# Mask tables, a granule's work list, the last granule's products and two output stores rearranged in an attention-plus-MLP kernel

## The chip, the cores and the metric

The kernel runs on one core of a Trainium2 chip. The metric is the device time of that core in microseconds (us). Every kernel was executed several times; the first execution of each was also profiled (for the kernel before, one more execution beside the three that were timed). The time of an execution is about 1.8 us longer than the span that its trace shows (209.63 against 207.9 for the kernel before). All executions told of here are in the fast state, with a granted TensorE clock of 0.996 to 1.0.

## The reference, cut to what matters

```python
# q, k, v: (B=4, H=8, S=768, D=64);  n_global = 8, n_local = 96
scores = (q @ k.transpose(0, 1, 3, 2)) / sqrt(D)
keep = is_global | is_local            # first 8 keys, or 0 <= row - col < 96
scores = where(keep, scores - slope[h] * dist, -1e9)
a = softmax(scores)
x = (a @ v).transpose(0, 2, 1, 3).reshape(3072, 512)

h = x @ w_in                           # 512 -> 2048
g = s * maximum(h, 0)**2 + b
out = g @ w_out                        # 2048 -> 512, float32
```

## The kernel before

The 3072 rows are worked on in 12 *granules* of 256. For each granule PE (TensorE) makes the scores, ACT takes the Exp, DVE multiplies by a mask table (`tmpl`), PE makes the attention products, DVE normalises them into `xn`, and a transposing DMA makes `xT` of it (granules 4 to 11; for the earlier ones PE transposes it). Then come eight hidden-layer products `P1` (8 matmuls of 256 columns each, into one PSUM bank), ReLU on ACT, and a Square on ACT (`"act"`) or on DVE (else, or `"late"` with a later `Q`). The product with `w_out` is made plainly for granules 0 to 2 (`P2`), and as seven smaller products of sums and differences for the others (`W_mm`). Five PSUM pools matter: `psh` has two banks; `av`, `pso`, `scA` and `scB` serve one tile at a time.

The order of work is written by hand: each engine executes its instructions in the order in which the calls below issue them. The mask tables and their surroundings, before:

```python
    def make_tmpl(h):                          # a mask table: one Exp on ACT
        nc.scalar.activation(tmpl[:, h, :], base..., ACT.Exp, scale=slope)
    ...
    P1(1, 1)
    make_tmpl(2)
    P1(1, 2)
    make_tmpl(3)
    P1(1, 3)
    P1(0, 6)
    make_tmpl(4)
    T_quads(2, "k", ("pso", "av"))             # PE transposes k of granule 2
    T_ev(2, 0, "k")                            # evictions: DVE
    T_ev(2, 1, "k", "act")                     #            ACT
    P1(0, 7)
    T_quads(2, "q", ("pso", "av"))
```

One attention product `A`, with its normalisation, and the list that granules 3 and 4 are woven from:

```python
    def A(j, hp, tag="av", norm=True):
        ...                                    # 8 matmuls into a tile of pool `tag`
        if norm:
            A_norm(j, hp)                      # DVE: reciprocal, product into xn
            flush()                            # DVE: the Square that is pending

    def period(j, items, at, late=None, mid=()):
        SS(j, (0, 1))                          # scores and Exp
        run(items, at[0]);  A(j, 0)
        run(items, at[1]);  A(j, 1, "psh")
        run(list(mid), 100)
        SS(j, (2, 3))
        ...
        run(items, at[2]);  A(j, 2)
        KO(j + 1)                              # DVE copies of keys
        run(items, at[3]);  A(j, 3, "psh")
        if late is None:
            XT_dma(j)                          # two transposing DMAs, SP queue
        ...
        run(items, 100)
```

The last granule's seven products end with a product of eight 256-column matmuls, one addition on DVE and one store:

```python
        W_mm(j, 4)
        W_post(j, 4)
        nc.sync.dma_start(W_rows(j)[:, 1, lo], o[:, 1, lo])
```

The softmax here doesn't subtract the row's maximum and nothing guards it: scores larger than these inputs give would overflow.

## Time and profile before

| what | value |
|---|---|
| time, median of 3 executions | 210.44 us (210.06 to 210.52) |
| time of the execution that was traced | 209.63 us |
| span of the trace | 207.9 us |
| last matmul of the last product starts | 203.83 us |
| last store issued / landed / span ends | 204.66 / 206.53 / 207.86 us |

The lines of the profile on which the argument rests are in the prediction below, with how to read them. In the chain of waits the columns are start, duration, and what the time was spent on. In the order of time of one engine, a number in square brackets is the idle time before the instruction and names who ended it.

### The profile page before, as it was taken

Reading aid. Unit: us, or ns where it says so; the run is one execution under the profiler, and the core shown is the slowest. Engines: PE = TensorE matmul, PEld = TensorE weight load, DVE = VectorE, ACT = ScalarE, POOL = GpSimd, SP = SyncE. Lnnn points to the kernel's source line nnn. Section 1 sums busy time; section 2 is a strip of 40 time slices with the busy share of each in tenths; the row PEclk is TensorE's granted clock in tenths of the full one; section 3 lists DMA queues with packets and bytes.
Section 4 is the critical chain, followed back from the end, with each engine's and each line's share of the span. In section 5 each row is a group of like instructions: output and inputs, shape, how many; then the busy total and the mean of one; then the engine's idle time right before and its main releaser. Section 6 shows DMA issues by size and latency. Waiting matters only on the chain.

```text
span 207.9 us, 5598 instructions
## 1 busy us (share of the span) xinstructions
PE 200.8 (97%) x2291; PEld 160.8 (77%) x2291; DVE 167.9 (81%) x404; ACT 119.8 (58%) x184; POOL 75.5 (36%) x98
## 2 busy tenths in 40 slices
PE   7999999999999998999999999999999999999992
PEld 2667866557666777888988988988978988988882
DVE  3776567599889998788799799788799799787683
ACT  5779899345978784636536536546356456425300
POOL 8985673937364006509029019037000000000000
PEclk9999999999999999999999999999999999999999
DMA  5999999999999976999969959959946040040022
GB/s 165 193 184 198 188 196 190 182 145 160 134 131 166 182 133 85 183 144 132 209 93 118 208 83 119 207 101 120 193 79 176 3 151 4 0 151 3 2 104 101
DMA packets 103850, 27.64 MB, mean 133 GB/s; under 512 B 91408, under 2 KB 101904, under 8 KB 103824
## 3 DMA queue, kind: packets, MB, share of 16 engines
q0 software_dynamic: 70976, 13.11, 86.3%
q1 hardware_dynamic: 31792, 13.64, 32.1%
q10 hardware_dynamic: 1056, 0.52, 0.9%
q8 instruction: 18, 0.29, 0.6%
q14 instruction: 8, 0.07, 0.1%
HBM read 27.26 MB, written 6.29 MB: 161 GB/s over the span
## 4 chain that ended last, share of the span: by engine, by line
PE 79%; ACT 9%; DVE 5%; DMA 4%; issue 2%; SPq 0%; ACTq 0%; DVEq 0%
PE ps L528 35%; PE ps_w L690 14%; PE ps_wb L690 6%; PE ps L589 6%; PE ps_av L446 4%; PE ps_s L395 4%; PE ps_wa L690 3%; ACT pt L408 3%; ACT gT L538 2%; DMA xT<-xn 2%; DMA raw<-in_k_dram 2%; PE ps_s L379 2%; PE ps_2s L589 2%; DVE xn L464 1%; ACT gT L546 1%
## 5 line engine op out<-in xcount | busy, mean ns | idle before, releaser
L528 PE MATMUL ps<-xT,w_in_bf 128*128 128x256 bf16 x768 | 96.5, 273 | 1.0 <-DMA xT<-xn 0.6
L528 PEld LDWEIGHTS <-w_in_bf 128*128 128x128 bf16 x768 | 72.9, 98 | 12.4 <-DMA xT<-xn 0.9
L540 ACT ACTIVATE gT<-ps 128x512 bf16<-128x512 f32 x72 | 43.0, 598 | 59.1 <-PE ps L528 56.3
L408 ACT ACTIVATE pt<-ps_s 128x1024 bf16<-128x1024 f32 (+1 forms) x48 | 43.0, 952 | 2.0 <-PE ps_s L395 2.0
L690 PEld LDWEIGHTS <-sw 128*128 128x128 bf16 x288 | 28.1, 98 | 3.4
L418 DVE TENSOR_TENSOR pt<-pt,tmpl 128x1024 bf16<-128x1024 bf16 (+1 forms) x40 | 25.2, 647 | 2.9 <-ACT pt L408 2.4
L556 DVE TENSOR_TENSOR gT<-gT 128x512 bf16<-128x512 bf16 x66 | 25.1, 416 | 1.8 <-ACT gT L540 1.6
L690 PEld LDWEIGHTS <-gT 128*128 128x128 bf16 x216 | 20.5, 98 | 3.3 <-issue 0.2
L112 POOL DMA_DIRECT2D vaug<-in_v_dram x24 | 21.5, 911 | 4.1 <-DMA w_out_bf<-in_moe_w_out_dram 1.7
L125 POOL COPY pdum<-xT 1x1 bf16<-1x1 bf16 x5 | 4.7, 944 | 48.6 <-DMA xT<-xn 48.6
L464 DVE TENSOR_TENSOR xn<-ps_av,rc 128x256 bf16<-128x256 f32 x48 | 20.4, 425 | 1.7
L589 PE MATMUL ps<-w_out_bf,gT 128*128 128x512 bf16 x80 | 19.7, 379 | 0.0
L690 PE MATMUL ps_w<-tw,sw 128*128 128x256 bf16 x144 | 18.7, 272 | 0.0
L700 DVE SCALAR_TENSOR_TENSOR u<-ps_w,s_bc,bvec 128x256 f32<-128x256 f32 x27 | 12.9, 480 | 6.7 <-PE ps_w L690 6.7
L446 PEld LDWEIGHTS <-pt 128*128 128x128 bf16 x352 | 15.3, 98 | 3.3 <-DVE xn L464 1.0
L104 POOL DMA_DIRECT2D qnat<-in_q_dram x18 | 16.1, 905 | 2.8 <-DMA w_out_bf<-in_moe_w_out_dram 1.4
L538 ACT ACTIVATE gT<-ps 128x512 bf16<-128x512 f32 x24 | 14.2, 598 | 4.4 <-PE ps L528 4.4
L446 PE MATMUL ps_av<-vaug,pt 128*128 128x65 bf16 x224 | 16.4, 193 | 0.3 <-DVE xn L464 0.2
L104 POOL DMA_DIRECT2D knat<-in_k_dram x18 | 16.0, 894 | 1.2 <-issue 1.0
L463 DVE RECIPROCAL rc<-ps_av 128x4 f32<-128x4 f32 x48 | 8.7, 182 | 9.2 <-PE ps_av L446 9.0
L589 PEld LDWEIGHTS <-gT 128*128 128x128 bf16 x96 | 8.6, 98 | 8.2
L395 PE MATMUL ps_s<-qT,kT 64*128 64x128 bf16 x224 | 12.4, 218 | 0.0
(94 smaller groups left out, 241.1 us busy)
## 6 DMA issues: line engine op xcount, KB each, us to landing
out_dram<-o_pr SPq DMA_DIRECT2D x8, 512.0 KB, 4.1
vaug<-in_v_dram POOLq DMA_DIRECT2D x24, 128.0 KB, 7.8
knat<-in_k_dram POOLq DMA_DIRECT2D x22, 128.0 KB, 5.7
qnat<-in_q_dram POOLq DMA_DIRECT2D x22, 128.0 KB, 7.7
w_in_bf<-in_moe_w_in_dram POOLq DMA_DIRECT2D x8, 256.0 KB, 8.2
w_out_bf<-in_moe_w_out_dram POOLq DMA_DIRECT2D x4, 512.0 KB, 9.9
out_dram<-o_pr SPq DMA_DIRECT2D x7, 256.0 KB, 5.3
raw<-in_q_dram ACTq DMA_DIRECT2D x2, 256.0 KB, 4.9
```

The source lines that it names most:

```text
L104: nc.gpsimd.dma_start(t[:, i, :, :], src[b, :, sb * P : (sb + 1) * P, :].rearrange("h p d -> p h d"))
L112: nc.gpsimd.dma_start(vaug[b % 2][:, sb, :, 0:D], v[b, :, sb * P : (sb + 1) * P, :].rearrange("h p d -> p h d"),)
L395: nc.tensor.matmul(ps[:, hi, oc * P : (oc + 1) * P], lhsT=kt[r, :], rhs=qT[j][r, hp, i * P : (i + 1) * P], start=not biased, stop=not bias ...
L408: nc.scalar.activation(pt[:, :, 0:n], ps[:, :, 0:n], ACT.Exp, scale=QSCALE)
L418: nc.vector.tensor_tensor(pt[:, :, 0:n], pt[:, :, 0:n], m, ALU.mult)
L446: nc.tensor.matmul(av[:, i, hi, :], lhsT=pt[:, hi, c * P : (c + 1) * P], rhs=vv, start=n_ == 0, stop=n_ == len(ops) - 1,)
L464: nc.vector.tensor_tensor(xn[j][:, :, 2 * hp : 2 * hp + 2, :], av[:, :, :, 0:D], rc[:].to_broadcast((P, GB, 2, D)), ALU.mult,)
L528: nc.tensor.matmul(ps[:, i, :], lhsT=w_in_bf[:, kc, fc * P : (fc + 1) * P], rhs=xT[j][:, kc, :], start=(kc == 0), stop=(kc == KC - 1),)
L540: nc.scalar.activation(gs.rearrange("p f (r t) -> p f r t", r=2), ps[:].rearrange("p f (t r) -> p f r t", r=2), ACT.Relu,)
L556: nc.vector.tensor_tensor(gs, gs, gs, ALU.mult)
L589: nc.tensor.matmul(po[j, tb], lhsT=gT[j][:, fc, tb * P : (tb + 1) * P], rhs=w_out_bf[:, fc, :], start=(fc == 0), stop=(fc == FC - 1),)
L690: nc.tensor.matmul(wt[j, ps], lhsT=lhs[:, f, :], rhs=rhs[:, f, :], start=first and f == 0, stop=f == HF - 1, skip_group_check=True,)
```

## The change

Its intent is to take out places where PE stands still, and to shorten what follows the last product. It has four parts: (1) mask tables 2 to 5 are made later, the fourth attention product of granule 2 gets another bank; (2) in granules 3 and 4 three Squares move from ACT to DVE, one hidden-layer product moves behind the attention products, and the key copy after the last of them; (3) the last granule's products are reordered and its last product is made in two parts of 128 columns, each in its own bank, with its own addition and store; (4) the two stores of granule 0, and those of granule 2, become one each.

```diff
 # (1)
-    make_tmpl(2)                      # ... between P1(1, 1), P1(1, 2), P1(1, 3), P1(0, 6)
-    make_tmpl(3)
-    make_tmpl(4)
+    make_tmpl(2)                      # after P1(1, 3)
+    make_tmpl(3)                      # after the evictions of q
+    make_tmpl(4)                      # after VO(2);  make_tmpl(5): after P1(1, 7)
-    A(2, 3)
+    A(2, 3, "psh")
-    XT_pe(2, "act", "psh")
+    XT_pe(2, "act", "av")
 # (2)
         A(j, 2)
-        KO(j + 1)
+        if at[3]:
+            KO(j + 1)
         run(items, at[3])
         A(j, 3, "psh")
+        if not at[3]:
+            KO(j + 1)
 ...
-            (P1, 2, 4, "act"),
+            (P1, 2, 4),
 ...
-            ... (P1, m, 2, "act"), (P2, l, 6), (P1, m, 3, "act"), (P1, m, 4, "act")]
+            ... (P1, m, 2, "late"), (P1, m, 3, "late"), (P2, l, 6), (Q, m, 2), (Q, m, 3)]
+            items += [(P1, m, 4, "act"), ...
-            period(j, items, (4, 3, 3, 0), ...)
+            period(j, items, (4, 2, 3, 0), ...)
 # (3)  products 1, 2, 6, 5, 7, 0, 4  ->  1, 5, 6, 2, 7, 0, then product 4 as:
+        for e in range(2):
+            ps = ps_h.tile(..., tag="psh")[:, 0, 0:P]
+            cs = slice(e * P, (e + 1) * P)
+            for f in range(HF):
+                nc.tensor.matmul(ps, lhsT=g_blk(j, 1, 1)[:, f, :], rhs=tw[:, 3, f, cs], ...)
+            nc.vector.scalar_tensor_tensor(out=o[:, 1, cs], in0=ps, scalar=s_bc[:], in1=u4[:, cs], ...)
+            nc.sync.dma_start(W_rows(j)[:, 1, cs], o[:, 1, cs])
 # (4)
+    def P2_store_all(j):
+        nc.sync.dma_start(out[t0 : t0 + GT, :].rearrange("(i p) c -> p i c", p=P), o_t[j][:])
-            (P2_bias, 0, 0),
-            (P2_bias, 0, 1),
+            (P2_bias, 0, 0, False),
+            (P2_bias, 0, 1, False),
+            (P2_store_all, 0),
 ...                                   # and the same in P2_out, for granule 2
```

More of the change, by code (lines that the diff above doesn't have):

```diff
@@ L614, in P2_out @@
         )
-        t0 = b * S + g * GT + tb * P
-        nc.sync.dma_start(out[t0 : t0 + P, :], o_sb)
+        if tb == 1:
+            P2_store_all(j)
     raw = {}
@@ L629, in P2_bias @@
             P2_store(j, tb)
+    def P2_store_all(j):
+        b, g = bg(j)
+        t0 = b * S + g * GT
+        nc.sync.dma_start(
+            out[t0 : t0 + GT, :].rearrange("(i p) c -> p i c", p=P), o_t[j][:]
+        )
     def P2_store(j, tb):
@@ L671, in W_mm @@
         if n == 1:
-            wt[j, "a"] = ps_o.tile([P, DM], F32, name="ps_w", tag="pso")[:, 0:HC]
+            tag = "av" if j == NJ - 1 else "pso"
+            wt[j, "a"] = PS[tag].tile([P, DM], F32, name="ps_w", tag=tag)[:, 0:HC]
         elif n == 2:
@@ L675, in W_mm @@
         elif n == 5:
-            wt[j, "b"] = ps_b.tile([P, 2, DM], F32, name="ps_wb", tag="scB")[:, 0, 0:HC]
+            if j == NJ - 1:
+                t = ps_h.tile([P, 2, GT], F32, name="ps_wb", tag="psh")
+            else:
+                t = ps_b.tile([P, 2, DM], F32, name="ps_wb", tag="scB")
+            wt[j, "b"] = t[:, 0, 0:HC]
         elif n == 0:
@@ L750, in W_end @@
         W_post(j, 1)
+        W_mm(j, 5)
+        v = W_part(j, "u3")
+        W_add(j, v, "b", bvec[:, hi])
+        W_sw(j, 4)
+        W_mm(j, 6)
+        W_post(j, 6)
+        t = W_part(j, "t")
+        W_add(j, t, "b", wt[j, "u2"])
         W_mm(j, 2)
         W_post(j, 2)
-        W_mm(j, 6)
-        W_sw(j, 4)
-        W_post(j, 6)
-        W_mm(j, 5)
-        t = W_part(j, "u1")
-        W_add(j, t, "b", wt[j, "u2"])
         W_mm(j, 7)
-        W_post(j, 7)
-        W_post(j, 5)
+        W_add(j, o[:, 1, hi], "a", v)
+        u4 = W_part(j, "u1")
+        W_add(j, u4, "a", bvec[:, lo])
         nc.sync.dma_start(W_rows(j)[:, 1, hi], o[:, 1, hi])
@@ L765, in W_end @@
         nc.sync.dma_start(W_rows(j)[:, 0, :], o[:, 0, :])
-        W_mm(j, 4)
-        W_post(j, 4)
-        nc.sync.dma_start(W_rows(j)[:, 1, lo], o[:, 1, lo])
+        for e in range(2):
+            ps = ps_h.tile([P, 2, GT], F32, name="ps_e", tag="psh")[:, 0, 0:P]
+            cs = slice(e * P, (e + 1) * P)
+            for f in range(HF):
+                nc.tensor.matmul(
+                    ps,
+                    lhsT=g_blk(j, 1, 1)[:, f, :],
+                    rhs=tw[:, 3, f, cs],
+                    start=f == 0,
+                    stop=f == HF - 1,
+                )
+            nc.vector.scalar_tensor_tensor(
+                out=o[:, 1, cs], in0=ps, scalar=s_bc[:], in1=u4[:, cs], op0=ALU.mult, op1=ALU.add
+            )
+            nc.sync.dma_start(W_rows(j)[:, 1, cs], o[:, 1, cs])
     def P2(j, c, where=None):
@@ L856 @@
     P1(1, 1)
+    P1(1, 2)
+    P1(1, 3)
     make_tmpl(2)
-    P1(1, 2)
-    make_tmpl(3)
-    P1(1, 3)
     P1(0, 6)
-    make_tmpl(4)
     T_quads(2, "k", ("pso", "av"))
@@ L872 @@
     VO(2)
-    make_tmpl(5)
+    make_tmpl(4)
     P1(1, 5)
@@ L877 @@
     P1(1, 7)
+    make_tmpl(5)
     make_tmpl(6)
@@ L1074 @@
             items = [(P1, m, 0, "act"), (P2, l, 4), (P1, m, 1), (W_tw, 2, 0, 4)]
-            items += [(P2, l, 5), (P2_bias, 1, 0), (P1, m, 2, "act"), (P2, l, 6), (P1, m, 3, "act"), (P1, m, 4, "act")]
-            items += [(P2, l, 7), (P1, m, 5, "act"), (P1, m, 6), (W_tw, 4, 0, 4), (P1, m, 7), (W_sw, m, 3), (flush,), (W_tw, 4, 4, 8)]
-            period(j, items, (4, 3, 3, 0), mid=((W_tw, 2, 4, 8), (P2_bias, 1, 1, False)))
+            items += [(P2, l, 5), (P2_bias, 1, 0)]
+            items += [(P1, m, 2, "late"), (P1, m, 3, "late"), (P2, l, 6), (Q, m, 2), (Q, m, 3)]
+            items += [(P1, m, 4, "act"), (P2, l, 7), (P1, m, 5, "act"), (P1, m, 6), (W_tw, 4, 0, 4), (P1, m, 7), (W_sw, m, 3), (flush,), (W_tw, 4, 4, 8)]
+            period(j, items, (4, 2, 3, 0), mid=((W_tw, 2, 4, 8), (P2_bias, 1, 1, False)))
         else:
```

## The prediction

> **What bounds the kernel now.** I read the page first, then what ended PE's waits, then the chain of waits in three stretches, then the order of time on DVE, ACT and the store queue. The busy line of the page and the chain's shares:
>
> ```profile
> PE 200.8 (97%) x2291; PEld 160.8 (77%) x2291; DVE 167.9 (81%) x404; ACT 119.8 (58%) x184; POOL 75.5 (36%) x98
> ...
> PE 79%; ACT 9%; DVE 5%; DMA 4%; issue 2%; SPq 0%; ACTq 0%; DVEq 0%
> ```
>
> PE carries the span. The change takes no product away, so all it can win is time in which PE stands still, and what follows PE's last product. The 97% hides the stalls, since the matmul ends are modelled, so I took stalls as the distance between the starts of neighbouring matmuls, less what such a matmul normally takes. In the stages that the change touches they are few. First, the mask tables (21 to 41 us), from the chain of waits:
>
> ```profile
> 27.85 0.63 ACT tmpl L255
> 28.48 0.48 ACT kT L308
> 28.96 0.04 issue
> 29.00 0.44 PE ps_t L288 x30
> ...
> 40.00 0.44 DVE xn L464
> 40.43 0.05 issue
> 40.48 0.42 PE ps_av L446 x8
> ```
>
> A mask table on ACT (0.63) runs ahead of the eviction of the transposed k; PE, which needs that bank for the transposes of q, starts again at 29.00 where it stood at 28.50: 0.47 us lost. Another 0.22 is lost at 25.96 to 26.18, where two tables among the ReLU evictions keep a `psh` bank. At 39.92 to 40.48 the fourth attention product of granule 2 waits 0.35 for the normalisation of the third, whose bank it shares. Then the step from granule 4 to 5:
>
> ```profile
> 75.54 4.15 DMA xT<-xn
> 79.69 0.05 issue
> 79.74 1.92 PE ps L528 x16
> ```
>
> The second half of the transposed x lands at 79.69, and PE, which could have gone on at 78.97, starts at 79.74: 0.77 lost. Smaller stalls of this stage are 0.31 at 72.3, 0.23 at 77.9, and in granule 3 0.31 at 56.4, where a Square on ACT (55.56 to 56.19) delays a ReLU. What DVE does before the 72.3 stall:
>
> ```profile
> 69.64 0.68 DVE L651 TENSOR_TENSOR tw<-w_out_bf,tw 128x1024 bf16<-128x1024 bf16 x1
> 70.24 0.69 DVE L627 TENSOR_TENSOR o_pr<-o_pr,bvec 128x512 f32<-128x512 f32 x1
> 70.93 0.69 DVE L418 TENSOR_TENSOR pt<-pt,tmpl 128x1024 bf16<-128x1024 bf16 x1
> 71.85 0.69 DVE L418 TENSOR_TENSOR pt<-pt,tmpl 128x1024 bf16<-128x1024 bf16 x1 [0.22 <-ACT pt L408]
> ```
>
> The first mask product has no idle time before it: there DVE, not the Exp, is last; before the second it idles only 0.22. The end, in order of time:
>
> ```profile
> 203.07 1.04 PE L690 MATMUL ps_w<-tw,gT 128*128 128x256 bf16 x8
> 203.32 0.48 DVE L700 SCALAR_TENSOR_TENSOR o_pr<-ps_wd,s_bc,u 128x256 f32<-128x256 f32 x1
> 203.43 0.33 SPq L762 DMA_DIRECT2D out_dram<-o_pr  x1
> 203.85 0.38 SPq L765 DMA_DIRECT2D out_dram<-o_pr  x1
> 204.15 0.48 DVE L700 SCALAR_TENSOR_TENSOR o_pr<-ps_w,s_bc,bvec 128x256 f32<-128x256 f32 x1 [0.35 <-PE ps_w L690]
> 204.66 0.33 SPq L768 DMA_DIRECT2D out_dram<-o_pr  x1
> ```
>
> After the last product come one DVE addition of 0.48 and a store; the span ends at 207.86, 3.2 us after that store is issued.
>
> **What the Trainium skill says.** "TensorE: Matmul & The Clock Gate", section "Wait — 56ns, not 53.3ns?": warm matmuls start N/2.4 GHz plus about 2.5 ns apart, 109 ns at 256 columns and 56 at 128. The trace agrees: 8 products of 256 columns in 0.87 us, 8 transposes of 128 in 0.45. So two halves of 128 columns cost what one of 256 does. The same page's specification table calls ScalarE and VectorE strict FIFO: the k eviction stood behind a table whose result nobody needed yet. "PSUM — Partial Sum Buffer", section "PSUM bank collisions raise a hardware error": PE and DVE or ACT may not use one bank and quadrant together, so they are kept apart by bank; hence the waits at 28.5 and 40, and why the two column parts get a bank each. "DMA: Bandwidth & Descriptors", section "Anatomy of one DMA — SWDGE (gpsimd) path", gives about 2 us fixed per DMA, mostly the receipt of the last write. The last store (SP queue, 128 KB) landed 1.9 us after its issue, so cutting its bytes cannot remove most of it.
>
> **The change, part by part.**
>
> Mask tables. Eight tables stay eight. Tables 2 and 3 no longer stand between evictions, so the 0.22 goes. Table 4 no longer stands before the k eviction. I followed ACT onward with starts 0.48 apart after a ReLU or copy and 0.62 after a table: table 2 at 26.63, the ReLU 27.25, the k eviction 27.73 to 28.31, where PE arrives at 28.1. So some 0.1 stays, and PE is about 0.59 ahead. From there ACT is full up to the Exps (near 31.7 instead of 32.05); the ReLU behind them frees a `psh` bank about as PE asks for it, which leaves 0.57. Tables 5, 6 and 7 follow, three of 0.62, done near 36.3, when the next scores are there: no loss. The fourth attention product gets a `psh` bank: 0.35 more. Sum 0.92.
>
> Granule 3. One Square moves from ACT (0.63) to DVE (0.42), into an idle gap of 0.41 at 55.75. The ReLU starts about 0.24 earlier, and PE with it: 0.20.
>
> Granule 4 (times as before, without what is won upstream, which shifts all engines alike). One hidden-layer product (8 matmuls, 0.87) moves behind the attention products, two Squares go from ACT to DVE, behind the normalisations, and the key copy (0.42 + 0.18) moves behind them too. The Exps come some 1.8 us earlier. But DVE's row up to the first mask product is the same as before: 70.93 to 71.62, the second to 72.25. So the last attention product, for which PE would be ready near 71.4, starts near 72.3, 0.3 earlier than now, not 1.2. A second new wait, for a `psh` bank until the second normalisation (69.7) where PE arrives at 69.4, is contained in it. The transpose is issued at about 73.5 instead of 74.29 and, even with the slow 4.15, lands near 79.0. PE then has the moved 0.87 to fill its time and reaches the product that needs x at 72.55 + 0.87 + 5.89 = 79.31, without waiting (72.55 is the end of that attention product, 0.25 long; 5.89 is what PE does today from its end, 72.85, to 78.97, less the 0.23 stall). Gain 79.74 - 79.31 = 0.43, out of 1.31 us of stalls here: the wait moves from the DMA to DVE.
>
> Tail. PE's time is equal. The last addition shrinks from 0.48 to about 0.35 (by 1 ns a column, from 480 ns at 256 and 740 at 512), so the last issue is near 204.53 instead of 204.66. But the 256 KB store ahead of it moves only by 0.06, and its packets and those of the two small ones run back to back. I allow 0.1.
>
> Merged stores. Two issues fewer on a queue that is off the chain, the same bytes; the 256 KB of granule 2 now go out together at 82: 0.
>
> Sum 0.92 + 0.20 + 0.43 + 0.10 = 1.65; 210.44 - 1.65 = 208.79. Each stage can give back some, so I say 208.9.
>
> **The rivals.** (a) All stalls of these stages go: 1.04 + 0.31 + 1.31 and the tail 0.3, 2.96 in all: 207.5. The Exps and the DMA indeed come early enough; against it speaks DVE's row without idle time from 67.0 to 71.6. (b) The gain is given back to loads: q of granule 3 lands transposed at 50.67, and PE first reads it at 51.68, so PE can come only 1.0 earlier there; the merged store may delay the next transposes of x. That leaves about half: 209.6. (c) DVE is made the bound: three Squares of 0.42 and a late key copy in granules 3 and 4 hold up granule 5 too, which eats the 0.43: 209.3 or so. DVE's 81%, and 3.85 busy of 5 us at 80 to 85, speak against a lasting delay.
>
> **Range and chances.** The centre is the sum with a small discount; (a) with half its excess gives the low end, (b) the high end: 208.2 to 209.7. Over 2% would need 4.2 us, more than every stall named here, so faster has 0.02; slower would need a new stall of 4 us, which nothing hints at: 0.01.
>
> **What would show it.** Right: no PE wait for kT evictions or before the last attention product of granule 2; PE near 0.9 us ahead at 40 us and about 1.1 ahead at 57; the wait for xT gone; DVE named as what releases the attention products of granule 4; the last DVE addition 0.35 and the span's end about 3.2 to 3.3 us after it is issued to the store queue. Wrong: PE not ahead at 51.7 (loads bind), a wait for xT that is still there or has moved to granule 5, or no DVE wait in granule 4 and 0.9 us more won than I say.

## The result, and the profile after

The changed kernel took **207.86 us** (median of 4 executions, 207.70 to 208.04), beside 210.25 (209.66 to 210.52) for the kernel before in the same rounds. The ratio is **0.989** (95% interval 0.9866 to 0.9915). Ratios here are the mean time of one kernel's fast executions over that of the other's of the same rounds, so not quite the ratio of the medians. That is within 2%, as said; but 207.86 lies 0.34 us below the low end of the range, 208.2. The prediction of the time was wrong: the change gave more than I said. All outputs are right.

The page of the changed kernel, its busy line and the shares of the chain:

```profile
PE 199.9 (97%) x2291; PEld 161.0 (78%) x2299; DVE 169.1 (82%) x409; ACT 118.3 (57%) x181; POOL 73.7 (36%) x98
...
PE 83%; DVE 8%; ACT 3%; DMA 3%; issue 1%; POOL 0%; SPq 0%; DVEq 0%; ACTq 0%; POOLq 0%
```

Both traces record 2291 matmuls. The changed program has eight more (the last product is two halves of eight, and the weight loads went from 2291 to 2299); eight records are missing in its trace. PE's share of the chain rose from 79 to 83%, ACT's fell from 9 to 3%, DVE's rose from 5 to 8%. The span is 205.9 us instead of 207.9. The stretch of the mask tables, from the chain of waits:

```profile
26.85 0.37 PE ps_t L288 x32
27.22 0.98 PE ps L528 x8
28.20 0.48 PE ps_t L288 x32
...
38.40 0.42 PE ps_av L446 x8
38.81 0.86 PE ps L589 x4
39.68 0.24 PE ps_av L446 x8
```

No table and no eviction (`kT`) stands in the chain any more: PE goes straight from the transposes of k to a hidden-layer product and to the transposes of q. The fourth attention product follows at 39.68 without a wait for a normalisation. Granule 4, again from the chain of waits:

```profile
69.85 1.22 DVE pt L418 x2
71.06 0.05 issue
71.11 0.42 PE ps_av L446 x8
...
73.52 2.53 DMA xT<-xn
76.05 0.02 issue
...
76.43 1.02 ACT pt L408
77.45 0.04 issue
77.49 1.03 PE ps_wa L702 x8
78.52 1.53 PE ps L528 x14
```

As the prediction said, DVE's two mask products now release the last attention products, in place of the Exps. The transposed x is there at 76.05 after 2.53 us, where it took 4.15; PE comes to it only then, at 78.52 in the chain (by the matmul's own start 78.36). Before 77.49 PE stands still for `scA`, the bank that the next granule's Exps free. The end, in order of time on DVE and on the store queue:

```profile
202.35 0.80 DVE L792 SCALAR_TENSOR_TENSOR o_pr<-ps_e,s_bc,u 128x128 f32<-128x128 f32 x2
```

```profile
202.84 0.88 SPq L795 DMA_DIRECT2D out_dram<-o_pr  x2
```

The two additions follow each other, and so do the two issues: the last store is issued at 203.32, when the queue is through with the issue of the one ahead. The span ends 2.6 us later; before, it ended 3.2 us after the last issue. This is the first surprise: the last store landed in 1.69 us instead of 1.87, and the end came 0.93 us after that landing instead of 1.33.

I then measured the two traces stage by stage, by when certain matmuls start, and did the same for every experiment. Each number is how much longer (+) or shorter a stage is than in the first trace of the kernel before:

```
stage            begins at (us, first trace of before)
start            0       until PE's first hidden-layer product
loads            12.84   until the first transpose of k of granule 2
tables           27.15   until the first product of granule 1 with w_out in a score bank
granule 3        40.74   until the bias product
granule 4        61.42   until PE is through with the moved work
xT               78.09   until the hidden-layer products of granule 4 begin
granule 5        79.74   until the second of its seven small products
rest             95.03   until the last matmul starts
tail             203.83  until the last store has landed
end              206.53  until the span ends, at 207.86

                 start loads tables  g.3   g.4    xT   g.5  rest  tail   end | span
before_again     +0.25  0     0     +0.01 +0.01   0     0   +0.06  0     0   | 208.17
merge_only       -0.30 +0.80  0      0     0    +0.08 +0.80 +0.07  0   -0.36 | 208.95
tail_only         0     0     0      0     0    -0.02  0    +0.26 -0.23 -0.04 | 207.84
tables_only      -0.30 +0.58 -0.60   0    +0.01 +0.05  0    -0.23  0     0   | 207.36
granules_only    +0.45  0     0    -0.09  +0.46 -0.77 -0.01 -0.23 -0.01 +0.01 | 207.67
after (first)    -0.15 -0.22 -0.61 -0.09  +0.46 -0.77 -0.01 +0.10 -0.23 -0.41 | 205.93
after_again      +0.24 -0.21 -0.60 -0.09  +0.47 -0.77 -0.01 -0.16 -0.23 -0.41 | 206.09
after_third      -0.28 -0.09 -0.61 -0.09  +0.46 -0.77 -0.01 +0.08 -0.24 -0.42 | 205.89
after_unmerge1   +0.15 -0.21 -0.60 -0.09  +0.46 -0.77 +0.15 +0.02 -0.24  0.00 | 206.74
```

Some stages repeat to 0.02 us; others come and go whatever the kernel is: the start (-0.30 to +0.45), a wait for a part of `w_in` under "loads", and waits for the transposed x under "granule 5" and "rest". In "rest", 0.06 to 0.08 us of the changed kernels are no loss: the last matmul has 128 columns and starts later within its product. I count that against the tail, which leaves -0.15 to -0.17 there; 0.15 is used below.

### The profile page after: what moved, and what is told of

It is laid out like the page before. It is cut to its first block, busy times and chain, and to the rows that moved or that the text cites. A ratio compares the mean times of both kernels' runs of the same rounds, so it can differ in the third digit from the quotient of the medians.

```text
span 205.9 us, 5605 instructions
## 1 busy us (share of the span) xinstructions
PE 199.9 (97%) x2291; PEld 161.0 (78%) x2299; DVE 169.1 (82%) x409; ACT 118.3 (57%) x181; POOL 73.7 (36%) x98
## 4 chain that ended last, share of the span: by engine, by line
PE 83%; DVE 8%; ACT 3%; DMA 3%; issue 1%; POOL 0%; SPq 0%; DVEq 0%; ACTq 0%; POOLq 0%
PE ps L528 37%; PE ps_w L702 14%; PE ps_wb L702 6%; PE ps L589 6%; PE ps_av L446 5%; PE ps_s L395 5%; PE ps_wa L702 4%; ACT pt L408 2%; DMA raw<-in_k_dram 2%; PE ps_s L379 2%; DVE xn L464 2%; PE ps_2s L589 2%; DVE pt L418 2%; DMA xT<-xn 1%; DVE o_pr L627 1%
## 5 line engine op out<-in xcount | busy, mean ns | idle before, releaser
L556 DVE TENSOR_TENSOR gT<-gT 128x512 bf16<-128x512 bf16 x68 | 25.8, 415 | 1.8 <-ACT gT L540 1.6
L702 PEld LDWEIGHTS <-gT 128*128 128x128 bf16 x208 | 19.7, 98 | 3.2 <-issue 0.2
L125 POOL COPY pdum<-xT 1x1 bf16<-1x1 bf16 x5 | 3.0, 595 | 49.3 <-DMA xT<-xn 49.3
L589 PE MATMUL ps<-w_out_bf,gT 128*128 128x512 bf16 x74 | 18.8, 379 | 0.4 <-issue 0.2
L589 PEld LDWEIGHTS <-gT 128*128 128x128 bf16 x96 | 8.8, 98 | 8.1
```

Of the source, the lines that this page charges most:

```text
L556: nc.vector.tensor_tensor(gs, gs, gs, ALU.mult)
L589: nc.tensor.matmul(po[j, tb], lhsT=gT[j][:, fc, tb * P : (tb + 1) * P], rhs=w_out_bf[:, fc, :], start=(fc == 0), stop=(fc == FC - 1),)
L702: nc.tensor.matmul(wt[j, ps], lhsT=lhs[:, f, :], rhs=rhs[:, f, :], start=first and f == 0, stop=f == HF - 1, skip_group_check=True,)
```

## The experiments

Sixteen runs of ten different kernels were made on four chips (0, 2, 13, 14). The expectations carry their theories in their own words. Two recur below: the *look-through theory* (theory 1 in the expectations), that the gain beyond the prediction stands at the end, after the last landing, and hangs on the number of DMAs; and the *fetch theory* (theory 3), that the quick or slow transpose of x hangs on a fetch of instructions in flight beside it.

### First call: the end of the kernel (chip 0)

**The kernel before, unchanged** (no edit).

> The kernel before, unchanged. Theory 1 (the missed gain is a fixed property of the program, among it 0.43 us at the end, where the sync engine looks at eight DMA semaphores one after another and the last store's is the first of them): ratio 1.000; in this trace too the end comes about 1.33 us after the last store's landing. Theory 2 (the profile that I read was a lucky execution, 209.63 against a median of 210.25 to 210.44): the single runs scatter by 0.5 us or more, and this trace, if it is of a longer run, shows extra PE stalls of 0.4 to 0.8 us that the first trace doesn't have, most likely before a product that reads transposed x or q.

Measured: 209.72 us (209.22 to 210.21) beside 209.57; ratio 1.0007 (0.9991 to 1.0023). Two copies of one kernel differ by under 0.2%. The single executions scatter by 1.0 us, as theory 2 said, but the traced one (210.03) shows no wait of 0.4 us or more that the first trace lacks: +0.25 in the start, +0.06 in the rest. On this chip the kernel before was some 0.7 us quicker than the 210.25 of the first comparison.

**The stores merged, nothing else.**

```diff
-            (P2_bias, 0, 0),
-            (P2_bias, 0, 1),
+            (P2_bias, 0, 0, False),
+            (P2_bias, 0, 1, False),
+            (P2_store_all, 0),
 ...
-        nc.sync.dma_start(out[t0 : t0 + P, :], o_sb)
+        if tb == 1:
+            P2_store_all(j)
```

> Only the four stores of granules 0 and 2 merged into two. Prediction on record: 0. Theory 1: two DMAs fewer on the hardware queues shift the rotation of their eight semaphores by two, so the last store's is now the last but one that the final look-through comes to; the end comes some 0.96 us after the last landing instead of 1.33, 0.37 us faster, ratio 0.998, and PE's last product is not earlier. Theory 2 (merging relieves the DMA queues or the transposes): PE's last product earlier by 0.3 us or more, the end as before.

Measured: 209.95 us (209.31 to 210.72) beside 209.57; ratio 1.0021 (1.0001 to 1.0041). The end stage is 0.36 shorter, as the look-through theory (next paragraph) has it, yet the kernel isn't quicker. The traced execution, the slowest, shows why: it loses 0.80 waiting for x of granule 5, and another 0.80 waiting for `w_in`. Granule 5's transposing DMAs took from issue to landing, between 84 and 97 us, first before, then in this kernel:

```profile
DMA to landing us min/median/max: 3.3/3.7/4.1
```

```profile
DMA to landing us min/median/max: 4.9/5.3/5.7
```

The merged store of granule 2 was issued at 83.79 and landed at 89.74, where the second of two small ones had landed at 87.42; so it still lay beside those transposes. That fits the second half of my rival (b), but doesn't show it: the same transposes took 5.21 and 4.35 in a later trace of the kernel before, without any merged store (`before_look1`), and 4.40 and 3.61 in after, with it.

**The look-through theory.** After its last store the SP queue looks at eight semaphores of its DMAs, one after the other, in a fixed order, and only then ends the kernel. In the trace of before the looks stand at 206.54, 206.60, 206.67 and so on to 206.97, about 0.06 us apart, after the landing at 206.53. After the change, the last look stands at 205.02, right after the landing at 205.00. The DMAs take the eight semaphores in turn. Before issues 73 of them on the SP and ACT queues, so the last store uses the semaphore that is looked at first, and seven looks follow its landing. After issues 72 (two fewer by the merges, one more by the split tail); its last store uses the one looked at last, and nothing follows. What the SP queue waited for at the kernel's last line (total, times, longest), before, after, and in `merge_only` with 71 DMAs:

```profile
SPq L1150 <- DMA out_dram<-o_pr: 1.5, 1, 1.5
```

```profile
SPq L1182 <- DMA out_dram<-o_pr: 0.8, 3, 0.4
```

```profile
SPq L1158 <- DMA out_dram<-o_pr: 1.1, 2, 0.6
```

Before, one long wait at the first semaphore is followed by looks that wait for nothing; after, the waits are several and short, since the other semaphores are looked at while the last store is still on its way.

**The changed kernel, unchanged.**

> The changed kernel once more, for comparison on one chip. Both theories: ratio 0.989 within 0.002, scatter of the single runs 0.4 us or less; the end some 0.9 us after the last landing.

Measured: 207.75 us (207.39 to 207.96) beside 209.57; ratio 0.9911 (0.9898 to 0.9923), 1.8 us. That is less than the first comparison's 2.4, and the expectation missed narrowly: 0.9911 where 0.989 within 0.002 was said, a scatter of 0.57 us where 0.4 was said. The end came 0.93 us after the last landing, as said.

**The changed kernel with granule 0's stores apart again** (73 DMAs, as before).

```diff
-            (P2_bias, 0, 0, False),
-            (P2_bias, 0, 1, False),
-            (P2_store_all, 0),
+            (P2_bias, 0, 0),
+            (P2_bias, 0, 1),
```

> The changed kernel with the two stores of granule 0 apart again (one DMA more), all else as changed. Theory 1: the last store falls back on the semaphore that is looked at first, and the end comes 0.43 us later after its landing (1.33 instead of 0.9): time 0.4 us above the changed kernel, PE's last product at the same time. Theory 2: no difference at the end; whatever difference there is stands in PE's stalls near 75 to 80 us.

Measured: 208.28 us (208.0 to 208.51); ratio 0.9937 (0.9926 to 0.9949), against 0.9911 for the changed kernel in the same rounds. The intervals don't touch. The end stage is back at its old length (0.00 instead of -0.41), and the median is 0.53 longer, of which the trace puts 0.41 at the end and 0.16 at granule 5's x. One more store near 65 us, whose landing nothing waits for before the end, costs 0.4 us at the end, through the place of the last store in a rotation. With 71, 72, 73 and 74 DMAs the end stage was 0.98, 0.90 to 0.93, 1.33 to 1.36 and 1.30 us in all the traces.

### Second call: each part by itself (chip 2)

**The tail alone** (the edits to `W_mm` and `W_end` only).

```diff
-            wt[j, "a"] = ps_o.tile([P, DM], F32, name="ps_w", tag="pso")[:, 0:HC]
+            tag = "av" if j == NJ - 1 else "pso"
+            wt[j, "a"] = PS[tag].tile([P, DM], F32, name="ps_w", tag=tag)[:, 0:HC]
 ...  # and part (3) of the change
```

> Only the order of the last granule's products and the last product in two parts. My steps: PE's time equal, last addition 0.35 instead of 0.48, last store issued 0.13 earlier, landing 0.1 to 0.2 earlier. By theory 1 one DMA more moves the last store to the second semaphore looked at, 0.06 better. Together 0.2 us, ratio 0.999. Rival: the 256 KB store ahead keeps the DMA queue busy and nothing is won.

Measured: 209.42 us (209.19 to 209.76) beside 209.62; ratio 0.9988 (0.9975 to 1.0). The trace has 0.23 in the tail (0.15 net of the later start of the last matmul) and 0.04 at the end, where 74 DMAs put the last store on the second semaphore looked at. But the last store is not issued 0.13 earlier, as expected: counted from the last matmul of the product before, it is issued after 1.72 us, where it was 1.70, and lands in 1.69 us instead of 1.87. Another 0.18 came in the "rest", a wait for x near 155 us, and hid the gain in the span of this execution.

**The tables alone.**

```diff
-    make_tmpl(2)      # and 3, 4, 5: each moved as in part (1) of the change
-    A(2, 3)
+    A(2, 3, "psh")
-    XT_pe(2, "act", "psh")
+    XT_pe(2, "act", "av")
```

> Only the mask tables moved and the fourth attention product of granule 2 in a bank of its own. My steps: PE ahead by 0.6 at 29 us and 0.92 at 41 us; that reaches the end: ratio 0.9955. Rival (loads give it back): PE not ahead at 52 us or at 80 us, ratio 0.998 or more. What the wait for xT at 75 to 80 us does decides how much is left after it.

Measured: 208.83 us (208.53 to 209.2) beside 209.62; ratio 0.9961 (0.9947 to 0.9975), 0.82 us. The executions form two groups, near 208.55 and near 209.1, so that the median meets the 0.82 of the stages partly by chance. The traced one is of the slower group; it waits 0.58 for `w_in`, where the 0.21 of the first stall was to be won, and shows the other 0.60 whole.

**Granules 3 and 4 alone.**

```diff
-        KO(j + 1)
+        if at[3]:
+            KO(j + 1)
 ...  # and the rest of part (2) of the change
```

> Only the rearrangement in granules 3 and 4 (Squares, one hidden-layer product, key copy). My steps: 0.20 in granule 3 and 0.43 in granule 4, 0.6 us in all, ratio 0.997. If the kernel before often waits longer for xT than its first trace shows (theory 2), this part takes that wait away and is worth more, 1.0 us and above, ratio 0.995 or less.

Measured: 209.5 us (209.07 to 209.83) beside 209.62; ratio 0.9991 (0.9979 to 1.0004). The trace has -0.09 in granule 3 and +0.46 - 0.77 = -0.31 in granule 4, together 0.40, the same to 0.01 as in the whole change. The timed 0.19 (0.0009 x 209.62) is less than that, and its interval, 0.44 faster to 0.08 slower, just holds 0.40: the load waits vary by as much.

**The changed kernel with one addition moved.** The chain of waits of after had a bias addition of 0.60 in front of the mask products (69.25 to 69.85). Here it goes to the end of granule 4's list.

```diff
+            items += [(P2_bias, 1, 1, False)]
-            period(j, items, (4, 2, 3, 0), mid=((W_tw, 2, 4, 8), (P2_bias, 1, 1, False)))
+            period(j, items, (4, 2, 3, 0), mid=((W_tw, 2, 4, 8),))
```

> The changed kernel with one of DVE's bias additions (0.68) moved from before granule 4's mask products to the end of that granule's list. My theory that DVE sets the attention products there: the last of them starts 0.6 us earlier or until PE or a bank is last, PE at its own pace near 70.5 instead of 71.1, and 0.3 to 0.5 us are won if the moved addition does not hold up granule 5. Rival: DVE is short of time until 80 us anyway and the addition only moves the wait: within 0.1 us of the changed kernel.

Measured: 207.71 us (207.06 to 208.56) beside 209.62; ratio 0.9908 (0.9887 to 0.993). Three executions took 207.06 to 207.32, three took 208.1 to 208.56. The chain of waits of the traced one, 207.26:

```profile
69.78 0.81 PE ps L589 x3
70.59 0.49 PE ps_av L446 x16
71.08 0.87 PE ps L528 x8
```

The two attention products run back to back, without DVE in the chain, and granule 4 is 0.42 shorter than in after. That shows that DVE was the bound there. The median does not move.

### Third call: what made the transpose slow (chip 13)

The transposed x of granule 4 took 4.15 us before and 2.53 after. In all traces of the first two calls, the second of its two DMAs took either about 2.5 or over 4. What told the two apart was a fetch of instructions: 18 DMA packets of 16 KB on queue 8, in every trace.

```profile
q8 instruction: 18, 0.29, 0.6%
```

The columns below are when the fetch near that transpose starts, when the transpose is issued, when it lands, and the time between; the upper block was known before this call, the lower one is of this call.

```
run                    fetch  issued  landed  took
before                 77.26   75.54   79.69  4.15
before_again           77.53   75.79   79.95  4.16
merge_only             77.06   76.03   80.27  4.24
tail_only              77.24   75.53   79.67  4.14
tables_only            77.00   75.23   79.43  4.20
granules_only          77.36   74.95   77.42  2.47
after                  76.30   73.52   76.05  2.53
after_again            76.40   73.94   76.46  2.52
after_unmerge1         76.20   73.85   76.34  2.49
after_dve_light        75.71   73.38   75.91  2.53

before_fetch_shift     73.04   77.52   79.98  2.46
after_third            75.88   73.53   76.07  2.54
after_dve_light_again  75.51   73.54   77.95  4.41
stores_rearranged      75.45   73.40   78.00  4.60
```

The transpose is due to land 2.5 us after its issue. In the table above, where a fetch starts 1.03 to 2.05 us after the issue, the transpose takes 1.6 to 2.1 us more; where the fetch starts 2.33 us after it or later, or is over before it, it does not. From before to after the issue came forward by 2.0 us (75.54 to 73.52) and the fetch by only 1.0 (77.26 to 76.30); the transpose slipped out ahead of it.

**The kernel before, with the fetches moved.** To start PE's fetches elsewhere, the idle matmuls at the start of the kernel become 57 instead of 9.

```diff
-    idle(9, "av")
+    idle(5, "av")
+    idle(52, "av", 8)
```

> The kernel before with 48 more (tiny) matmuls in the warm-up at its very start, 96 PE instructions in all, nothing else. In every trace of a kernel with the old order of granule 4 one 16 KB instruction fetch (DMA queue 8) begins near 77.0 to 77.5 us, while the second half of the transpose of x is in flight, and that half takes 4.1 to 4.2 us to land; with the new order it has landed before the fetch, in 2.5 us. Theory 3 (the fetch holds up the transpose): 96 PE instructions more bring the fetch forward to about 73 us of the old clock, before the transpose; the half lands in 2.5 us, and the stage from the second product of granule 3's output to the first hidden product of granule 4 is 0.77 us shorter (0.87 instead of 1.65). Rival (the loads and stores before it, or the place in the queue, make it slow): still 4.1 us and 1.65. The warm-up itself may cost a few tenths before 13 us, so I judge by the stage, not by the total.

Measured: 210.49 us beside 209.78; ratio 1.0032 (1.0011 to 1.0053). The start is 1.99 us longer in the trace, from the added matmuls; 0.77 of it comes back in the stage "xT" and 0.18 in the "rest". The fetch is now at 73.04, over four us before the issue, and both halves of the transposed x land quickly. Between 70 and 82 us, from issue to landing, first before, then this kernel:

```profile
DMA to landing us min/median/max: 2.4/3.3/4.2
```

```profile
DMA to landing us min/median/max: 2.4/2.4/2.5
```

The stage "xT" is 0.77 shorter, as expected, all other stages up to it repeat to 0.01, and "granule 5" to "end" change by under 0.2. One doubt is that everything after the start stands 2 us later against the loads. The pair `after_dve_light` and `after_dve_light_again` has no such doubt: one kernel, fetch at 75.71 and transpose 2.53, fetch at 75.51 and transpose 4.41. And the moved fetches made other transposes slow, where no load is left: one starts at 182.73, in granule 11's two transposes, which took 3.66 and 3.25. In the other 17 traces no fetch lies there, and they took 2.39 to 2.42 and 2.46 to 2.54. Up to the landing of the first of them, no other DMA was in flight beside them.

The later transpose of granule 9, issued near 150, follows the same rule in the 17 traces with fetches in their old places: 4.00 to 4.46 where the fetch starts 1.92 to 2.29 us after the issue, 2.46 to 2.48 where it starts 2.31 us after. From 4.19 on PE waits for that x near 155; this makes most of what comes and goes in the "rest".

**The version that might beat both.** The kernel with the moved addition, and with granule 2's stores apart and granule 1's merged, to keep the large store away from granule 5's transposes and the number of DMAs at 72.

```diff
-        if tb == 1:
-            P2_store_all(j)
+        t0 = b * S + g * GT + tb * P
+        nc.sync.dma_start(out[t0 : t0 + P, :], o_sb)
 ...
-            P2_store(1, 1)
+            P2_store_all(1)
 ...
-            items += [(P2, l, 5), (P2_bias, 1, 0)]
+            items += [(P2, l, 5), (P2_bias, 1, 0, False)]
```

> The changed kernel with the lighter DVE of granule 4, the two stores of granule 2 apart again and those of granule 1 merged in their place, so that the number of DMAs stays and the last store keeps the semaphore looked at last. If the merged 512 KB store of granule 2 is what delays the transposes of granule 5's x in some executions (0.8 us of wait in the merge-only run), the transposes land earlier than 91.75 in this trace, by 0.4 us or more, and the single runs lose their upper group (208.1 to 208.6): median 207.3 or less. Rival: the upper group comes from elsewhere, and stays.

Measured: 207.49 us (207.09 to 208.09) beside 209.78; ratio 0.9892 (0.9872 to 0.9913). The best median of all, but its interval overlaps that of the changed kernel in the same rounds (next but one), so it isn't shown to beat it. Its expectation missed: granule 5's transposes landed at 92.64, not before 91.75, one execution took 208.09, and the median is above 207.3. The traced execution still waited 0.31 for x of granule 5, with the large store gone: that the large store alone makes the slower executions has no support. The transpose of granule 4 was slow here (4.60), and cost only 0.11: in this kernel PE has other work until 77.94.

**The kernel with the moved addition again.**

> The kernel with the lighter DVE once more, on the same chip as the one above. Both groups of runs again (near 207.2 and 208.3) if its second group is a property of the program; if this trace falls in the slow group it shows where: by my theory a wait of 0.5 us or more before the first hidden product of granule 5 (near 93 us); by the rival near 21 us, where a load of w_in is late.

Measured: 207.72 us (207.14 to 207.91) beside 209.78; ratio 0.9902 (0.9885 to 0.9919). The trace keeps the 0.42 in granule 4 and loses 0.48 in granule 5, for x. That is the wait near 93 us that was expected (0.5 or more); the group near 208.3 did not come again. A fetch lies beside granule 5's transposes in every trace that I looked at, quick or slow, so it doesn't tell them apart. In `before_fetch_shift` none does, and they took 4.42 and 3.57. The cause of this wait is open.

**The changed kernel, third time.**

> The changed kernel a third time, for comparison on the same chip with the two above: 207.7 within 0.2, ratio to before 0.991; the lighter DVE is 0.4 us faster than it in the fast executions.

Measured: 207.69 us (207.61 to 208.21) beside 209.78; ratio 0.9909 (0.9892 to 0.9926), as expected. The fastest execution of the lighter DVE is 0.47 below its fastest, but the medians are equal (207.72 and 207.69), so the 0.4 is shown in granule 4 and not in the time.

### Fourth call: how much "before" varies (chip 14)

By the ratios, the first comparison gave a gain of 2.3 us (0.011 of 210.25), the later ones 1.9. Is a wait of about half a microsecond to be seen in slower executions of before?

> The kernel before, unchanged, for one more trace. If what the prediction missed lies partly in taking the gain of a fast execution (209.63) from a median of slower ones (210.44), an execution of 210.0 us or more shows waits of PE that the first trace does not have, 0.4 to 0.8 us: near 21 us for a load of w_in, or near 93 us for x of granule 5. Rival: a slow execution is slow outside the profiled span, or everywhere alike.

Measured: 209.53 us; span 207.77. It differs from the first trace by +0.24 in granule 5, -0.23 in the rest.

> As the first of these looks: an execution of 210.0 us or more shows a wait near 21 or near 93 us, and an execution near 209.2 shows neither of them.

Measured: 210.03 us (209.78 and 210.28); the traced one is the 209.78. It shows +0.12 in "loads", +0.06 in granule 5 and +0.10 in the rest, where the whole wait for x near 155 is 0.33. Nothing of half a microsecond. The slow execution was not the profiled one, so this did not settle it.

> The changed kernel, for one more trace. If the change also takes away waits that only some executions of the kernel before have, this shows none near 21 us and 93 us; if they come and go with the loads whatever the kernel, an execution of 208.0 or more shows one of them here too.

Measured: 207.61 us beside 209.43; ratio 0.9914 (0.9885 to 0.9943).

> As the first look at the changed kernel: an execution of 208.0 us or more would show a wait near 21 or near 93 us if such waits come and go whatever the kernel; an execution near 207.6 shows neither.

Measured: 207.82 us; ratio 0.9924 (0.9895 to 0.9953). Both lie with the other executions of the changed kernel.

## Why the prediction was right or wrong

**Against which number I subtracted.** I read stalls out of one trace, of an execution that took 209.63, and subtracted them from a median of 210.44. Nothing in the trace accounts for the 0.8 between them. From 209.63 the same sum gives 209.63 - 1.65 = 207.98, with a range around it that would have held 207.86. This step put the result outside the range. (So did the next one: with its 0.41 the range would have begun at 207.8.) Later medians of before were 209.43 to 209.78, so 210.44 was high; what made the first chip's executions of before half a microsecond longer stays open.

**"Merged stores ... the same bytes ...: 0."** This term failed. It measured 0.41: the number of DMAs moved the last store to the semaphore that is looked at last. `after_unmerge1` takes the gain back with one store more. The check that I named, a span that ends 3.2 to 3.3 us after the last issue, came out wrong in the telling way: 2.6, of which the rotation gives 0.41 of the 0.6 gained and a quicker landing the rest. The text also calls granule 2's merged store 256 KB; it is two halves of 256 KB, 512 KB in all.

**Mask tables, 0.92.** Measured 0.21 + 0.61 = 0.82, by mechanism as said; `tables_only` timed 0.82, in executions that also lost or won other waits. The missing 0.1 seems to be in the attention products of granule 2, as read from the trace and not tested: the first starts 0.76 earlier than before, the second only 0.63, since it shares a bank with the first and waits for its normalisation.

**Granule 3, 0.20.** Measured 0.09. I had the ReLU start 0.24 earlier. Its line before, then after:

```profile
56.09 0.58 ACT L538 ACTIVATE gT<-ps 128x512 bf16<-128x512 f32 x1
```

```profile
55.01 0.60 ACT L538 ACTIVATE gT<-ps 128x512 bf16<-128x512 f32 x1 [0.46 <-PE ps L528]
```

PE was 0.98 ahead here, so 55.01 is 55.99 in the times of before: 0.10 earlier. ACT was free in time, but the matmuls that the ReLU reads were not done. PE still waits 0.22 of the former 0.31.

**Granule 4, 0.43.** Measured 0.31. DVE was the bound, as the prediction said: the last attention product starts 1.48 us earlier, 1.07 of it before this granule (0.15 of that in the start, which the change doesn't touch), so 0.41 by itself (said: 0.30). PE also gave up the wait for x. What I had wrongly dropped is the 0.23 for the bank `scA`: it is still there, at 77.49. (0.43 + 0.11 - 0.23 = 0.31.) The slow transpose, which I carried forward at 4.15 to be careful, was 2.53; at 4.15 it would have landed at 77.67, still before PE comes to it, because the moved product fills PE's time. In `stores_rearranged`, where PE comes to it earlier, 4.60 cost 0.11.

**Tail, 0.10.** Measured about 0.15, but not by the path that I gave, so the agreement is luck. The last addition took 0.35 as worked out and ended 0.11 earlier, counted from the last matmul of the product before. The last store was not issued earlier for that (after 1.72 us, before 1.70): I had left out that the queue was still issuing the first half's store, 0.38 us. The gain came from the landing, 1.69 us for 64 KB instead of 1.87 for 128 KB. Whether the bytes alone make that difference is not shown.

**The sum.** 0.82 + 0.09 + 0.31 + 0.15 + 0.41 = 1.78, where 1.65 was predicted, and the later rounds show 1.6 to 1.9 (one minus the ratios 0.9911, 0.9909, 0.9914 and 0.9924, times the medians of before). Two errors nearly cancel: the four named gains measured 1.37 against 1.65, and the end that I had at zero gave 0.41.

**Alone and together.** Timed alone, the parts give +0.44 for the stores, -0.25, -0.82 and -0.19, together -0.82, and the whole -1.87 (each is one minus the ratio, times the median of before). By stages they do add up. What doesn't add are the waits for loads and for x, which appeared in three of the four part kernels' traces (0.80 + 0.80, 0.18, 0.58) and not in those of the whole.

**Rivals.** Rival (a), that all stalls go, falls, though its 207.5 lies about as near to 207.86 as the low end of my range: the banks and DVE held as said. Rival (b) shows at most in single executions (the late x of granule 5, whose cause is open), not as half of the gain. Rival (c) falls: granule 5 is as long as before to 0.01 in the traces of after.

## What to carry to other kernels

A gain read from one trace belongs to that execution: subtract it from its own time, not from a median that stands elsewhere. The last landing is not the end: see what the queue does after it, and on which semaphore the last store falls, before writing down that a DMA more or less costs nothing. When one DMA takes much longer than its like, look at what else is in flight, instruction fetches too, and test it by moving that.

## What the Trainium skill lacked or had wrong

- "Runtime: NRT & Kernel Launch", section "Instruction fetch mechanics", says that instructions are refilled in blocks of 16 KiB by a DMA, at a cost that is "mostly hidden". The block size agrees (18 packets, 0.29 MB). It lacks what the fetch does to others: transposes with a fetch in flight took 4.14 to 4.60 us instead of 2.5 (granule 4's second one), which cost PE 0.77 us in the kernel before.
- "DMA: Bandwidth & Descriptors", section "DMA Transpose (X-bar)", treats what must not be in flight beside a transpose, as a matter of correct results; that a fetch beside it slows it by 1.6 to 2.1 us is not there.
- The end of a kernel: no page that I found tells that the queue looks at its eight DMA semaphores in a fixed order, about 0.06 us each, so that 72 DMAs on the SP and ACT queues end 0.41 us sooner after the last landing than 73.
